# Weight conversion of the first MoE layer placed behind the gate steps of its first six units

## The chip, the cores and the metric

The kernel runs on one core of one Trainium2 chip. The metric is the device time of one execution in microseconds (us); the kernel before was run three times, and its median is 710.7 us (707.14 to 711.53).

## The reference

Three layers follow one another. Clustered attention over 2 x 8 heads of 768 tokens gives 1536 tokens of 512 numbers. Then come two feed-forward layers ("MoE" layers); the first is the one around the change:

```
h = x @ w_in                      # 1536 x 512 times 512 x 2048
P = a[0] + a[1]*h + a[2]*h^2 + a[3]*h^3
Q = 1 + |b[0]|*|h| + |b[1]|*h^2
g = P / (Q + 1e-06)
x = g @ w_out                     # 1536 x 2048 times 2048 x 512
```

The second layer is x @ w_in2, a softmax-weighted product with a layer norm, and a product with w_out2. The weights of both layers arrive as float64.

## The kernel before

**Units.** The first MoE layer is cut into 48 units, each one block of 512 tokens (j) and one block of 128 hidden columns (f). Units 0 to 7 take j = 0 and f = 0 to 7, units 8 to 15 the same f for j = 1, units 16 to 31 all sixteen f for j = 2, units 32 to 47 f = 8 to 15 for j = 1 and then j = 0. A unit is made of five pieces:

- `ff_h` (line 710): TensorE (PE) makes h, 12 matmuls into one PSUM bank (128x512, names h0, h1, ...). There are four such banks, so the h of unit u + 4 can begin only when the bank of unit u is free. That is after `y L750` of unit u, which reads it last.
- `ff_g1` (line 732), the first gate step: ScalarE (ACT) makes t = |h| (L734) and y = a3*h + a2 (L735), GpSimd (POOL) makes q from t in two operations (L736, L737), VectorE (DVE) two operations on y and h (L738, L739).
- `ff_g2` (line 742): ACT takes Ln (L745) and Exp (L746) of q, writing over the h bank, and DVE finishes the quotient in three operations (L748, L749, L750).
- `ff_g3` (line 752): ACT rounds y to gh (L755), POOL makes the rest gl = y - gh (L756).
- `ff_y` (line 761), two units later (LAG = 2): PE adds gh and gl times w_out to four PSUM banks, again 12 matmuls. Two of them use gh alone and stand ahead of the first that needs gl.

**Weights.** Each block f of weights is 128 x 1024 numbers: columns 0 to 511 are for `ff_h`, 512 to 1023 for `ff_y`. It is converted in two halves, half 0 and half 1. One half goes through `to_f32` and `to_parts`: a transfer of 512 KB into a raw tile (L118), two ACT operations (L128 and L131), one DVE operation that puts the pieces together (L135), one ACT rounding (L139, the tile w1h) and one POOL difference (L140, the tile w1l). `to_f32` and `w1_parts` are generators that stop at each `yield`; four steps are one half. Blocks 0 to 4 (NPRE = 5) are converted during attention. Blocks 5 to 11, 14 halves in all, are converted during the first units: `bg` is the list of their generators, `run_bg(4)` (line 699) takes four steps. The raw tiles rotate through three buffers (`cv1`), the joined tiles w1w through two (`cw`).

**What sets the order.** Each engine works through its own queue in order. The order in the queue is set by the compiler's scheduler, which lists an instruction when its own estimate of time says that it is ready, in the order of the program otherwise. The program can hold instructions back with edges of order alone: `tc.issue_after(ins)` queues everything that its block puts on the engine of `ins` behind `ins`, and leaves other engines and the DMA queue (SP) free.

The main loop before the change is this:

```python
run_bg(4)
...
for u in range(NU + LAG):
    if 1 <= u <= NU:
        ff_g2(u - 1)
    if u < NU:
        hp = ff_h(u)
        ff_g1(u, hp)
    if 1 <= u <= NU:
        ff_g3(u - 1)
    ...
    if u >= LAG:
        ff_y(u - LAG)
    run_bg(4)
```

Of the kernel before, what the change touches and what calls it, by code (L numbers as in the profile page):

```python
# [10 lines left out]
AF = mybir.ActivationFunctionType  # L11
# [19 lines left out]
def fused_kernel(ctx: ExitStack, tc: tile.TileContext, qT, kT, v, cent, w1, w2i, w2o, gln, coef, centT, cst, out):  # L31
    nc = tc.nc
# [51 lines left out]
    NPRE = 5  # L84
# [18 lines left out]
    cv = [None]  # L103
# [9 lines left out]

    def to_f32(w, src, nm, early=False):
        raw = cv[0].tile([128, 512], mybir.dt.uint64, name=f"raw{nm}", tag="raw")
        nc.sync.dma_start(out=raw, in_=src)  # L118
        yield
        words = raw.bitcast(U32).rearrange("p (n two) -> p n two", two=2)  # L120
        lo, hi = words[:, :, 0], words[:, :, 1]
        wf, wu = w, w.bitcast(U32)

        nc.scalar.activation(out=wf, in_=hi.bitcast(F32), func=AF.Prelu, scale=2.0 ** -112, alpha=-(2.0 ** 32))  # L128


        nc.scalar.activation(out=lo, in_=lo, func=AF.Identity, scale=2.0 ** -29 * (1 - 2.0 ** -16), bias=less)  # L131
        if early:
            yield
        yield
        nc.vector.scalar_tensor_tensor(wu, wu, 3, lo, op0=ALU.logical_shift_left, op1=ALU.bitwise_or)  # L135
        yield
# [28 lines left out]
    raw, vv = {}, {}  # L165
    last = {}
# [528 lines left out]
    a0, a1, a2, a3 = (coef_t[:, i:i + 1] for i in range(4))  # L695
# [3 lines left out]
    def run_bg(k):  # L699
        while k and bg:  # L700
            try:
                next(bg[0])
                k -= 1
            except StopIteration:
                bg.pop(0)
# [26 lines left out]
    def ff_g1(u, hp):  # L732
        t, q, y = T("t", u), T("q", u, bufs=2), T("y", u, bufs=3)
        nc.scalar.activation(out=t, in_=hp, func=AF.Abs)  # L734
        nc.scalar.activation(out=y, in_=hp, func=AF.Identity, scale=a3, bias=a2)  # L735
        nc.gpsimd.tensor_scalar(q, t, ab[:, 1:2], ab[:, 0:1], op0=ALU.mult, op1=ALU.add)  # L736
        nc.gpsimd.tensor_tensor(q, q, t, op=ALU.mult)  # L737
        nc.vector.tensor_tensor(y, y, hp, op=ALU.mult)  # L738
        nc.vector.scalar_tensor_tensor(y, y, a1, hp, op0=ALU.add, op1=ALU.mult)  # L739
        live[u] = (q, y, hp)  # L740
# [167 lines left out]
    NTT = TOK // 128  # L908
    LAG = 2
    NU = len(ff_units)  # L910
    run_bg(4)
    turn[0] += turn[0] % 2
    h2 = []
    for u in range(NU + LAG):
# [4 lines that stand above are left out]
# [10 lines left out]
            h2.append(t_h(order[u - NU]))  # L929
        if u >= LAG:  # L930
            ff_y(u - LAG)
        run_bg(4)

    run_bg(10 ** 6)
    m1.close()
# [57 lines left out]
```

## Time and profile before

| what | value |
|---|---|
| median of three runs | 710.7 us |
| the profiled execution, its own time | 709.8 us |
| span of that execution in the trace | 708.0 us |
| PE busy | 624.2 us, 88% of the span |
| DVE busy | 500.0 us, 71% |
| ACT busy | 437.8 us, 62% |
| POOL busy | 393.2 us, 56% |
| PE's share of the chain that ended last | 35% |
| first matmul of the first MoE layer | at 273.35 us |
| first matmul of the second MoE layer | at 553.74 us |

The profile is one execution recorded on the chip. Times in it count from the start of the span. A row gives an engine, the line of the kernel, the operation with what it writes and reads, and how often. The idle time of an engine just before a row is put down to the instruction (its releaser) that ended it. The granted clock is the share of TensorE's full clock that the chip gave: 1.00 stands for 2.4 GHz and 0.50 for 1.2 GHz. The shares of busy time are means over attention and two MoE layers with different limits, so what this change is worth has to be read in its own stretch, from 273 us on.

### The profile page before, as it was taken

Reading aid. Unit: us, or ns where it says so; the run is one execution under the profiler, and the core shown is the slowest. Engines: PE = TensorE matmul, PEld = TensorE weight load, DVE = VectorE, ACT = ScalarE, POOL = GpSimd, SP = SyncE. Lnnn points to the kernel's source line nnn. Section 1 sums busy time; section 2 is a strip of 40 time slices with the busy share of each in tenths; the row PEclk is TensorE's granted clock in tenths of the full one; section 3 lists DMA queues with packets and bytes.
Section 4 is the critical chain, followed back from the end, with each engine's and each line's share of the span. In section 5 each row is a group of like instructions: output and inputs, shape, how many; then the busy total and the mean of one; then the engine's idle time right before and its main releaser. Section 6 shows DMA issues by size and latency. Waiting matters only on the chain.

```text
span 708.0 us, 13757 instructions
## 1 busy us (share of the span) xinstructions
PE 624.2 (88%) x5517; PEld 493.4 (70%) x5517; DVE 500.0 (71%) x648; ACT 437.8 (62%) x796; POOL 393.2 (56%) x363
## 2 busy tenths in 40 slices
PE   6777888777687868699999999899999899999998
PEld 3555666656466647476888877778888688888887
DVE  4779779788876872889776789878679765444450
ACT  2536556666566664998866798978668434444341
POOL 8554546483848743899765999898579500000000
PEclk9778889899788988799999999999999999999999
DMA  9963393847547224443100144330010000000001
GB/s 242 278 162 85 95 263 91 200 134 193 153 120 190 63 61 140 140 139 107 43 1 0 44 136 124 114 119 1 1 31 0 1 1 15 31 31 15 20 26 44
DMA packets 22439, 64.71 MB, mean 91 GB/s; under 512 B 4532, under 2 KB 5640, under 8 KB 22376
## 3 DMA queue, kind: packets, MB, share of 16 engines
q1 hardware_dynamic: 21944, 63.67, 32.0%
q8 instruction: 43, 0.70, 0.4%
q10 hardware_dynamic: 432, 0.17, 0.1%
q14 instruction: 20, 0.16, 0.1%
HBM read 59.16 MB, written 3.19 MB: 88 GB/s over the span
## 4 chain that ended last, share of the span: by engine, by line
PE 35%; DVE 7%; ACT 7%; DMA 5%; POOL 5%; issue 3%; ACTq 0%; DVEq 0%; POOLq 0%
PE hh L849 9%; PE o L900 9%; PE y L773 8%; PE h L721 6%; DMA raww<-in_w 2%; DMA rawv<-in_w2i 2%; DVE w1w L135 2%; PE lt L882 1%; POOL q L737 1%; POOL gl L756 1%; ACT y L735 1%; ACT h L745 1%; DVE xhl L616 1%; DMA rawv<-in_w2o 1%; ACT t L734 1%
## 5 line engine op out<-in xcount | busy, mean ns | idle before, releaser
L721 PE MATMUL h<-xhl,w1h 128*128 128x512 f32 x384 | 125.3, 404 | 10.8 <-DVE y L750 8.7
L401 ACT ACTIVATE p<-s,m 128x768 f32<-128x768 f32 x96 | 86.1, 898 | 77.8 <-DVE m L388 77.4
L388 DVE TENSOR_REDUCE m<-s 128x1 f32<-128x768 f32 x96 | 89.5, 944 | 40.8 <-PE s L383 40.6
L377 PE MATMUL s<-k,q 128*128 128x384 f32 x192 | 65.7, 429 | 46.3 <-ACT p L401 45.5
L721 PEld LDWEIGHTS h<-xhl,w1h 128*128 128x128 f32 x384 | 74.0, 194 | 29.7 <-DVE y L750 8.1
L428 PE MATMUL pv<-pt,v 32*64 32x192 f32 x3072 | 88.6, 373 | 1.4 <-issue 1.3
L418 DVE STREAM_TRANSPOSE pt<-p 128x1536 f32<-128x1536 f32 x48 | 84.6, 1763 | 0.0
L377 PEld LDWEIGHTS s<-k,q 128*128 128x128 f32 x192 | 34.9, 219 | 69.6 <-ACT p L401 56.3
L428 PEld LDWEIGHTS pv<-pt,v 32*64 32x64 f32 x3072 | 67.5, 153 | 19.4 <-issue 11.1
L773 PE MATMUL y<-gl,w1h 128*128 128x512 f32 x192 | 76.0, 396 | 3.8 <-POOL gl L756 3.8
L756 POOL TENSOR_TENSOR gl<-y,gh 128x512 fp32r<-128x512 f32 x48 | 68.6, 1430 | 18.8 <-ACT gh L755 18.7
L721 PE MATMUL h<-xhl,w1l 128*128 128x512 f32 x192 | 77.3, 404 | 0.0
L773 PE MATMUL y<-gh,w1l 128*128 128x512 f32 x192 | 75.4, 393 | 0.0
L773 PE MATMUL y<-gh,w1h 128*128 128x512 f32 x192 | 69.2, 395 | 0.0
L737 POOL TENSOR_TENSOR q<-q,t 128x512 f32<-128x512 f32 x48 | 64.5, 1344 | 3.2
L738 DVE TENSOR_TENSOR y<-y,h 128x512 f32<-128x512 f32 x48 | 32.9, 685 | 43.0 <-ACT y L735 42.7
L383 PE MATMUL s<-k,q 128*128 128x384 f32 x192 | 57.8, 388 | 2.3 <-DVE k L579 2.3
L736 POOL TENSOR_SCALAR q<-t,ab 128x512 f32<-128x512 f32 x48 | 42.5, 886 | 27.9 <-ACT t L734 19.2
L849 PE MATMUL hh<-vh,xhl 128*128 128x512 f32 x192 | 53.6, 393 | 1.3 <-ACT t L734 1.3
L494 POOL TENSOR_TENSOR xf<-u,rb 128x512 f32<-128x512 f32 (+1 forms) x14 | 13.8, 1006 | 66.0 <-DMA rb<-rd 66.0
L773 PEld LDWEIGHTS y<-gl,w1h 128*128 128x128 f32 x192 | 36.1, 188 | 15.1 <-POOL gl L756 7.2
L745 ACT ACTIVATE h<-q,qc 128x512 f32<-128x512 f32 x48 | 32.9, 685 | 20.0 <-POOL q L737 12.8
(151 smaller groups left out, 1361.0 us busy)
## 6 DMA issues: line engine op xcount, KB each, us to landing
raww<-in_w SPq DMA_DIRECT2D x32, 512.0 KB, 4.5
v<-in_v SPq DMA_DIRECT2D x64, 192.0 KB, 4.7
dup<-in_qT SPq DMA_DIRECT2D x31, 192.0 KB, 5.6
dup<-in_kT SPq DMA_DIRECT2D x31, 192.0 KB, 5.7
rawv<-in_w2i SPq DMA_DIRECT2D x8, 512.0 KB, 3.6
rawv<-in_w2o SPq DMA_DIRECT2D x8, 512.0 KB, 3.5
out<-ob SPq DMA_DIRECT2D x11, 256.0 KB, 2.0
pr<-in_qT SPq DMA_DIRECT2D x7, 384.0 KB, 5.9
```

The costliest lines, as they stand in the source:

```text
L377: r = nc.tensor.matmul(sp[:, a, 0:384], lhsT=q1[i][:, sl], rhs=k1[i][:, a * 384:(a + 1) * 384], start=True, stop=False)
L383: last["pe"] = nc.tensor.matmul(sp[:, a, 0:384], lhsT=q2[i][:, sl], rhs=k2[i][:, a * 384:(a + 1) * 384], start=False, stop=True)
L388: last["dve"] = nc.vector.tensor_reduce(m, sp[:, :, 0:384], axis=AX.XY, op=ALU.min)
L401: last["act"] = nc.scalar.activation(out=P[n, t // 2][:, t % 2], in_=sp[:, :, 0:384], func=AF.Exp, scale=-1.0, bias=m, accum_out=rs[key][: ...
L418: r = nc.vector.transpose(PT[n][:, 2 * i:2 * i + 2].rearrange("p t k -> p (t k)"), p.rearrange("p t a k -> p (t a k)"))
L428: last["pv"] = nc.tensor.matmul(pv[n][64 * c:64 * c + 64, r, 0:192].rearrange("p (t q) -> p t q", t=NT), lhsT=vv[n][sl, j], rhs=PT[n][sl, ...
L721: r = nc.tensor.matmul(hp, lhsT=w[:, kt * 128:(kt + 1) * 128], rhs=x[:, kt], start=(i == 0), stop=(i == 11))
L737: nc.gpsimd.tensor_tensor(q, q, t, op=ALU.mult)
L756: nc.gpsimd.tensor_tensor(gl, y, gh.bitcast(F32), op=ALU.subtract)
L773: nc.tensor.matmul(o, lhsT=w[:, c], rhs=g, start=(first and i == 0), stop=(last and i == 2))
L849: last["th"] = nc.tensor.matmul(hp[:, a], lhsT=y[:, kt], rhs=w[:, 512 * a:512 * a + 512], start=(kt == 0 and e == 0), stop=(kt == 3 and e ...
L900: r = nc.tensor.matmul(op[:, 0:m], lhsT=l[:, kt], rhs=w, start=(n == 0), stop=(n == 23))
```

## The change

Three things are edited. The loading of a raw tile is a function of its own, and the first three loads (both halves of block 5, half 0 of block 6) are issued by themselves ahead of the main loop, where a whole half was converted before (`run_bg(4)`). `ff_g1` notes its second ACT operation in `last["g"]`. And in units 0 to 5, `run_bg(4)` stands in a block that queues its ACT instructions behind that operation of the same unit.

```diff
+    raws = {}
+
+    def load_raw(src, nm):
+        raws[nm] = cv[0].tile([128, 512], mybir.dt.uint64, name=f"raw{nm}", tag="raw")
+        nc.sync.dma_start(out=raws[nm], in_=src)
+
     def to_f32(w, src, nm, early=False):
-        raw = cv[0].tile([128, 512], mybir.dt.uint64, name=f"raw{nm}", tag="raw")
-        nc.sync.dma_start(out=raw, in_=src)
+        if nm not in raws:
+            load_raw(src, nm)
+        raw = raws.pop(nm)
         yield
...
         nc.scalar.activation(out=t, in_=hp, func=AF.Abs)
-        nc.scalar.activation(out=y, in_=hp, func=AF.Identity, scale=a3, bias=a2)
+        last["g"] = nc.scalar.activation(out=y, in_=hp, func=AF.Identity, scale=a3, bias=a2)
...
     NU = len(ff_units)
-    run_bg(4)
+
+
+    for a in range(3):
+        load_raw(w1[NPRE + a // 2, :, 512 * (a % 2):512 * (a % 2) + 512], f"w1{NPRE + a // 2}{a % 2}")
     turn[0] += turn[0] % 2
...
             ff_y(u - LAG)
-        run_bg(4)
+        with tc.issue_after(last["g"].ins) if u < 6 else ExitStack():
+            run_bg(4)
```

The diff moves instructions on all engines from the first unit on; attention before it keeps its order, and so does the DMA queue. In the rows below the number after a name is the unit (t0, y1, q2) or the block and half (w1w50 is block 5, half 0; raww161 block 6, half 1); what stands behind the underscore is a running number. The lines of these operations are 7 higher in the changed kernel.

ACT at the start of the first MoE layer, before, from the second half of block 5 to the Ln of unit 0 (L745):

```order
L131 ACTIVATE raww151_3490<-raww151_3490,less_81 128x512
L139 ACTIVATE w1h5_3457<-w1w50_3459 128x512
L131 ACTIVATE raww160_3531<-raww160_3531,less_81 128x512
L139 ACTIVATE w1h5_3457<-w1w51_3489 128x512
L734 ACTIVATE t0_3480<-h0_3467 128x512
L735 ACTIVATE y0_3482<-h0_3467,coef_72 128x512
L128 ACTIVATE w1w60_3530<-raww160_3531 128x512
L131 ACTIVATE raww161_3584<-raww161_3584,less_81 128x512
L128 ACTIVATE w1w61_3583<-raww161_3584 128x512
L131 ACTIVATE raww170_3637<-raww170_3637,less_81 128x512
L139 ACTIVATE w1h6_3528<-w1w60_3530 128x512
L745 ACTIVATE h0_3467<-q0_3481,qc_3451 128x512
```

ACT at the same place, changed kernel, from its first instruction of the layer to the Exp of unit 0 (L753) and the t of unit 2:

```order
L741 ACTIVATE t0_3476<-h0_3463 128x512
L742 ACTIVATE y0_3478<-h0_3463,coef_72 128x512
L135 ACTIVATE w1w50_3487<-raww150_3457 128x512
L138 ACTIVATE raww150_3457<-raww150_3457,less_81 128x512
L741 ACTIVATE t1_3511<-h1_3498 128x512
L742 ACTIVATE y1_3513<-h1_3498,coef_72 128x512
L752 ACTIVATE h0_3463<-q0_3477,qc_3451 128x512
L135 ACTIVATE w1w51_3524<-raww151_3459 128x512
L138 ACTIVATE raww151_3459<-raww151_3459,less_81 128x512
L146 ACTIVATE w1h5_3485<-w1w50_3487 128x512
L753 ACTIVATE h0_3463<-h0_3463 128x512
L741 ACTIVATE t2_3548<-h2_3535 128x512
```

Seven conversion operations stood ahead of t0 and twelve ahead of Ln of unit 0; now there are none and two.

DVE at the start of the layer, before, up to `L750` of unit 0, which frees the first h bank:

```order
L135 SCALAR_TENSOR_TENSOR w1w50_3459<-w1w50_3459,raww150_3460 128x512
L135 SCALAR_TENSOR_TENSOR w1w51_3489<-w1w51_3489,raww151_3490 128x512
L738 TENSOR_TENSOR y0_3482<-y0_3482,h0_3467 128x512
L135 SCALAR_TENSOR_TENSOR w1w60_3530<-w1w60_3530,raww160_3531 128x512
L739 SCALAR_TENSOR_TENSOR y0_3482<-y0_3482,coef_72,h0_3467 128x512
L135 SCALAR_TENSOR_TENSOR w1w61_3583<-w1w61_3583,raww161_3584 128x512
L738 TENSOR_TENSOR y1_3517<-y1_3517,h1_3502 128x512
L739 SCALAR_TENSOR_TENSOR y1_3517<-y1_3517,coef_72,h1_3502 128x512
L748 SCALAR_TENSOR_TENSOR q0_3481<-q0_3481,h0_3467 128x512
L135 SCALAR_TENSOR_TENSOR w1w70_3636<-w1w70_3636,raww170_3637 128x512
L749 SCALAR_TENSOR_TENSOR h0_3467<-q0_3481,h0_3467 128x512
L750 SCALAR_TENSOR_TENSOR y0_3482<-y0_3482,coef_72,h0_3467 128x512
```

DVE at the same place, changed kernel, up to the same operation (now L757):

```order
L745 TENSOR_TENSOR y0_3478<-y0_3478,h0_3463 128x512
L746 SCALAR_TENSOR_TENSOR y0_3478<-y0_3478,coef_72,h0_3463 128x512
L142 SCALAR_TENSOR_TENSOR w1w50_3487<-w1w50_3487,raww150_3457 128x512
L745 TENSOR_TENSOR y1_3513<-y1_3513,h1_3498 128x512
L746 SCALAR_TENSOR_TENSOR y1_3513<-y1_3513,coef_72,h1_3498 128x512
L142 SCALAR_TENSOR_TENSOR w1w51_3524<-w1w51_3524,raww151_3459 128x512
L755 SCALAR_TENSOR_TENSOR q0_3477<-q0_3477,h0_3463 128x512
L756 SCALAR_TENSOR_TENSOR h0_3463<-q0_3477,h0_3463 128x512
L745 TENSOR_TENSOR y2_3550<-y2_3550,h2_3535 128x512
L757 SCALAR_TENSOR_TENSOR y0_3478<-y0_3478,coef_72,h0_3463 128x512
```

Five joins of weight halves stood ahead of the last gate operation of unit 0; now there are two, and one operation of unit 2 has come in between.

POOL at the start of the layer, before:

```order
L140 TENSOR_TENSOR w1l5_3458<-w1w50_3459,w1h5_3457 128x512
L140 TENSOR_TENSOR w1l5_3458<-w1w51_3489,w1h5_3457 128x512
L736 TENSOR_SCALAR q0_3481<-t0_3480,ab_3449 128x512
L737 TENSOR_TENSOR q0_3481<-q0_3481,t0_3480 128x512
L140 TENSOR_TENSOR w1l6_3529<-w1w60_3530,w1h6_3528 128x512
L736 TENSOR_SCALAR q1_3516<-t1_3515,ab_3449 128x512
L737 TENSOR_TENSOR q1_3516<-q1_3516,t1_3515 128x512
L140 TENSOR_TENSOR w1l6_3529<-w1w61_3583,w1h6_3528 128x512
```

POOL at the same place, changed kernel:

```order
L743 TENSOR_SCALAR q0_3477<-t0_3476,ab_3449 128x512
L744 TENSOR_TENSOR q0_3477<-q0_3477,t0_3476 128x512
L743 TENSOR_SCALAR q1_3512<-t1_3511,ab_3449 128x512
L744 TENSOR_TENSOR q1_3512<-q1_3512,t1_3511 128x512
L147 TENSOR_TENSOR w1l5_3486<-w1w50_3487,w1h5_3485 128x512
L743 TENSOR_SCALAR q2_3549<-t2_3548,ab_3449 128x512
L744 TENSOR_TENSOR q2_3549<-q2_3549,t2_3548 128x512
L147 TENSOR_TENSOR w1l5_3486<-w1w51_3524,w1h5_3485 128x512
L763 TENSOR_TENSOR gl0_3521<-y0_3478,gh0_3520 128x512
L743 TENSOR_SCALAR q3_3602<-t3_3601,ab_3449 128x512
L147 TENSOR_TENSOR w1l6_3576<-w1w60_3577,w1h6_3575 128x512
```

The q of units 0 and 1 now come before the first weight difference, and the weight differences stand about one to a unit.

On PE the order of the first units is h0 to h4, then y of unit 0, h5, the two leading matmuls of y of unit 1, h6, the rest of y of unit 1, y of units 2 and 3, h7, the two leading matmuls of y of unit 4, one matmul of h8, the rest of y of unit 4, then h8 and h9 mixed. Before it was h4, y of unit 0, h5, y of unit 1, h6, y of unit 2, h7, y of unit 3, h8 with y of unit 4, h9. Further on, y of units 16, 17 and 18 come in a row between the first matmul of h21 and the rest of it, where before y of unit 18 stood behind h22. The scheduler's order differs in places through the rest of the first MoE layer too, with the same instructions.

## Rows read from the trace of the kernel before

**Rows 1.** Page, busy times of the engines over the whole span.

```profile
PE 624.2 (88%) x5517; PEld 493.4 (70%) x5517; DVE 500.0 (71%) x648; ACT 437.8 (62%) x796; POOL 393.2 (56%) x363
```

**Rows 2.** Waits of PE from 265 to 600 us: total, times, longest.

```profile
PE h L721 <- DVE y L750: 8.7, 3, 6.5
PE y L773 <- POOL gl L756: 3.8, 7, 0.9
```

**Rows 3.** Timeline of PE: start us, us, operation, idle before and its releaser.

```profile
277.05 0.63 PE L721 MATMUL h<-xhl,w1l 128*128 128x512 f32 x1
...
285.88 0.40 PE L721 MATMUL h<-xhl,w1l 128*128 128x512 f32 x1
...
292.80 1.22 PE L721 MATMUL h<-xhl,w1h 128*128 128x512 f32 x2 [6.52 <-DVE y L750]
...
298.09 0.88 PE L773 MATMUL y<-gh,w1h 128*128 128x512 f32 x2
```

**Rows 4.** Timeline of ACT, DVE and POOL from 277 to 293 us, first conversion to L750.

```profile
277.06 0.67 ACT L128 ACTIVATE w1w<-raww 128x512 f32<-128x512 f32 x1 [3.76 <-DMA raww<-in_w]
...
281.18 0.58 ACT L734 ACTIVATE t<-h 128x512 f32<-128x512 f32 x1
281.66 0.77 ACT L735 ACTIVATE y<-h,coef 128x512 f32<-128x512 f32 x1
...
283.65 1.61 POOL L737 TENSOR_TENSOR q<-q,t 128x512 f32<-128x512 f32 x1
...
285.51 0.62 ACT L139 ACTIVATE w1h<-w1w 128x512 fp32r<-128x512 f32 x1
286.03 0.67 ACT L745 ACTIVATE h<-q,qc 128x512 f32<-128x512 f32 x1
...
288.30 0.59 ACT L746 ACTIVATE h<-h 128x512 f32<-128x512 f32 x1
...
291.99 0.75 DVE L750 SCALAR_TENSOR_TENSOR y<-y,coef,h 128x512 f32<-128x512 f32 x1
```

**Rows 5.** Busy time by stretch: PE, PEld, DVE, ACT, POOL; then granted clock, DMA share, GB/s.

```profile
286.20:292.80 6.60, 0.08 (x2) 0.00 (x1) 4.59 (x6) 6.43 (x12) 5.08 (x5) 0.67 0.44 140
292.80:298.10 5.30, 5.30 (x13) 4.15 (x14) 5.08 (x7) 5.30 (x11) 5.22 (x5) 0.50 0.47 171
298.10:340.00 41.90, 40.04 (x168) 31.08 (x167) 37.63 (x49) 38.11 (x66) 40.26 (x32) 0.99 0.38 126
340.00:400.00 60.00, 60.00 (x263) 48.90 (x262) 41.48 (x61) 42.08 (x70) 39.20 (x34) 1.00 0.00 1
400.00:480.00 80.00, 76.36 (x321) 60.62 (x320) 65.09 (x86) 69.20 (x119) 74.25 (x61) 0.98 0.39 119
```

**Rows 6.** Two shorter waits in PE's timeline, and the clock after each by stretch.

```profile
335.14 0.50 PE L773 MATMUL y<-gl,w1h 128*128 128x512 f32 x1 [0.86 <-POOL gl L756]
...
457.79 0.70 PE L721 MATMUL h<-xhl,w1h 128*128 128x512 f32 x2 [1.97 <-DVE y L750]
...
335.00:337.00 2.00, 1.85 (x8) 1.56 (x9) 1.32 (x3) 2.00 (x5) 1.28 (x3) 1.00 0.80 254
...
459.00:460.00 1.00, 1.00 (x4) 0.79 (x3) 1.00 (x2) 0.81 (x2) 1.00 (x2) 0.53 0.00 0
...
462.00:463.00 1.00, 0.82 (x3) 0.28 (x1) 1.00 (x2) 0.96 (x2) 1.00 (x1) 0.76 0.78 320
```

**Rows 7.** Lines L135, L140, L737, L736, L756 from 276 to 345 us: ns min/median/max.

```profile
L135 DVE SCALAR_TENSOR_TENSOR w1w<-w1w,raww x16: 685/1112/1507, 278.4 to 334.6; 128x512 uint32<-128x512 uint32 x16
...
L140 POOL TENSOR_TENSOR w1l<-w1w,w1h x14: 1263/1300/1754, 280.2 to 330.8; 128x512 fp32r<-128x512 f32 x14
...
L737 POOL TENSOR_TENSOR q<-q,t x11: 1276/1300/1612, 283.7 to 340.0; 128x512 f32<-128x512 f32 x11
...
L736 POOL TENSOR_SCALAR q<-t,ab x11: 761/772/1813, 282.8 to 339.1; 128x512 f32<-128x512 f32 x11
...
L756 POOL TENSOR_TENSOR gl<-y,gh x9: 1287/1735/1749, 296.0 to 343.5; 128x512 fp32r<-128x512 f32 x9
```

## The prediction

> **What bounds the kernel now.** I read the busy times first: PE is busy for 624.2 us, far ahead of DVE, ACT and POOL [rows 1]. These are means over three layers, so I went on to the stretch that the diff moves, the first MoE layer. The table of stretches shows that PE is full there when nothing is late: from 340 to 400 us it is busy for all 60 us and runs 263 matmuls, 0.229 us each [rows 5]. A unit (24 matmuls) then costs 5.5 us, and the layer gets shorter only by what PE loses beside that. The waits of PE from 265 to 600 us name the losses: 8.7 us in three waits for `y L750` on DVE, one of them 6.5 us, and 3.8 us in seven waits for `gl L756` on POOL [rows 2].
>
> The long one is at the start. The last matmul of h3 begins at 285.88, the first of h4 at 292.80 [rows 3]: h4 needs the bank of h0, and `y L750` of unit 0 begins only at 291.99 [rows 4]. Yet h0 was complete at about 277.7 (its last matmul begins at 277.05, 0.63 us long [rows 3]). The timeline of ACT and DVE says where the 14 us between went. t of unit 0 starts at 281.18, 3.5 us after h0, behind the conversions. q is ready at 283.65 + 1.61 = 285.26. Ln follows at 286.03, but Exp only at 288.30, behind two operations of unit 1 and a weight rounding, and L750 at 291.99 [rows 4]. In PE's wait ACT is busy for 6.43 of 6.60 us [rows 5]. So the wait is made by a queue, not by a transfer.
>
> It costs twice: behind it the granted clock is 0.50 (1.2 GHz) from 292.80 to 298.10, for 13 matmuls [rows 5].
>
> **The change part by part.** Nothing is removed or added in work: 14 halves are converted before and after, with the same instructions. What moves is their place.
>
> *The three early transfers.* They have the same places in the DMA queue as before, and the first conversion began at 277.06 when its transfer ended [rows 4]. They are worth nothing by themselves; they make up for the removed `run_bg(4)`, so that the data lies ready when unit 0 asks for it.
>
> *The wait before h4 (first term).* I walk the new queues with durations from rows 4, and 0.1 us less from start to start where one ACT operation follows another (t at 281.18, 0.58 us long, y at 281.66). t0 starts at 277.8 (h0 complete), y0 at 278.3, the two conversion operations at 279.0 and 279.5. t1 must wait for h1, 280.8; y1 281.3. q0 is ready on POOL at about 280.7 (0.8 + 1.3 us behind t0), Ln0 comes behind y1, 282.0. Then two conversion operations and a rounding (282.6, 283.2, 283.8), Exp0 at 284.3, done at 284.9. On DVE L748 and L749 take 0.68 each, to 286.3; one operation of unit 2 stands before L750 (0.69), which runs from 286.9 to 287.65. h4 starts at 287.7 in place of 292.8. PE could have issued it at 285.88 + 0.23 = 286.11. So 6.69 us of loss become 1.6, a gain of **5.1 us**. Bounds: the second weight join stands just before L748 and takes 0.69 to 1.51 us [rows 7]; I have 0.75, so the gain is 4.3 at the least. It is 6.7 if nothing is late.
>
> *The clock behind it (second term).* From 292.80 to 298.09 the 12 matmuls of h4 took 5.29 us [rows 3]; at 0.229 they take 2.75. That is 2.54 us if the clock stays up. Two rows bracket a wait of 1.6 us: after an idle time of 0.86 us the clock stayed at 1.00; after one of 1.97 us it was at 0.53 about a microsecond later and 0.76 in the slice from 462 to 463 [rows 6], some 3.5 us at half speed, a loss of 1.75. My wait lies between them, so I take half of that loss, 0.85, and a gain of **1.7 us** (0.8 to 2.5).
>
> *The stretch behind (third term).* From 298.10 to 340 PE ran 168 matmuls [rows 5], 38.5 us at 0.229, so 3.4 us were lost in small waits and at the tail of the slow clock. The change spreads the 14 halves to about one per unit, up to unit 13. ACT is fine: t, y, Ln, Exp, gh and half a conversion are 3.2 + 2.05 us less eight overlaps of 0.1, 4.5 us of a unit's 5.5. POOL is close: by the medians L736, L737, L756 and L140 take 0.77 + 1.30 + 1.74 + 1.30 = 5.1 us [rows 7]. Walking POOL from the first weight difference (284.55, behind the rounding at 283.8) to half 0 of block 7 gives five L140, four each of the others, 21.7 us, done at 306.3. PE, full from 287.7 (h4, y0, h5, two matmuls, h6, the rest of y1, y2, y3: 84 matmuls, 19.2 us), wants that half for h7 at 306.9. It is just in time. Behind it come L736, L737, another L140 and gl of unit 4: 306.3 + 5.1 = 311.4, wanted at 310.4. That is 1.0 us lost there, and I allow another 0.9 for what such a walk does not see. 3.4 - 1.9 is a gain of **1.5 us**. Bounds: 3.4 if nothing is late; with POOL at its longest durations it turns into a loss (the rival below).
>
> A rule speaks against the change here. The Trainium skill, "GPSIMD Engine Reference", section 1 (Specifications), says that GpSimd shares its SBUF interfaces with VectorE and contends with VectorE instructions that have two SBUF inputs. The trace agrees: L135, with two such inputs, takes 0.69 us at the least and 1.11 in the median, gl 1.29 and 1.74 [rows 7]. By the rule, conversions that lie beside more gate steps keep both engines slow for longer; without it POOL's share of a unit would be its minima, 4.6 us, and the third term 3.4.
>
> *From 400 to 480 us (fourth term).* Blocks 12 to 15 and the second layer's weights are converted there. The scheduler's order differs, the work does not. PE ran 321 matmuls in 80 us, 73.5 at full rate: 6.5 us lost, with POOL busy for 74.25 [rows 5]. New small waits can come and old ones go; the wait of 1.97 us for L750 and its slow clock (3.7 us together) are among them [rows 6]. I take **0**, with 3.7 either way.
>
> *The sum* is 5.1 + 1.7 + 1.5 + 0 = 8.3 us. The profiled execution took 709.8, so 701.5 us; against the median of the runs, 710.7, that is 9.2 less (1.3%). About 1% (7.1 us, a time of 703.6) is what a measurement of this kernel tells from no change.
>
> **The rivals.**
>
> *More goes.* The wait at 457.79 falls too, since PE now makes y of units 16 to 18 together and has other work when a bank is late: 701.5 - 3.7 = 697.8, or 697.0 with the clock kept behind h4. For it: the order on PE there. Against it: POOL's 93% in that stretch. Chance 0.16.
>
> *The wait shrinks, but the rest gives back.* The first term is at its lower end, 4.3, the clock falls for a full 1.75 us, so that the second is 0.8, and the third is 0: 709.8 - 5.1 = 704.7. For it: the wait of 1.6 us is nearer to 1.97 than to 0.86. Against it: ACT has 1 us to spare in each unit. Chance 0.21.
>
> *POOL becomes the bound: slower.* At their longest durations the four operations cost POOL 1.81 + 1.61 + 1.75 + 1.75 = 6.9 us a unit [rows 7], 1.4 above PE's 5.5. Over the eight units 5 to 12 that is 11.2 us, and two falls of the clock add 3.5. The first two terms (6.8) and the 3.4 us lost before, which this replaces, stand against it: 709.8 - 6.8 - 3.4 + 14.7 = 714.3; with the 3.7 us of the fourth term on top, 718.0. It decides as soon as POOL's four operations take over 5.5 us in the mean. For it: the contention above. Against it: from 298.1 to 340 POOL was busy for 40.26 of 41.9 us, with the same halves crowded into it, and PE still lost only 3.4 [rows 5]. Chance 0.06.
>
> *The change does not do what it says.* If t0 were held by a transfer or by memory that is freed late, ACT would do as before: 709.8. For it: t0 is now the first ACT instruction that writes into memory freed by attention. Against it: the first half was written at 277.06, before h0 was complete [rows 4]. Chance 0.05.
>
> **How the numbers follow.** The forecast, 701.5, has 0.52; its own range is 699 to 704. With "more" (0.16) and "gives back" (0.21) the range is **697.0 to 707.0**: at the low end all of the first two terms with the fourth's gain, at the high end "gives back" with a loss of 2.3 in the fourth. It leaves out 0.11 for the last two rivals and some tails. Faster by over 1% means 703.6 or less: the forecast's 0.49, "more" 0.16, and 0.04 of "gives back", 0.69. Within 1%: 0.17 of "gives back", 0.03 of the forecast, 0.05 where nothing happens, and 0.03 from the slower rival, 0.28. Slower: 0.03.
>
> **What would show it.** In the trace of the changed kernel, t0 should start within 0.3 us of 277.8, Exp0 near 284.3, and h4 between 287 and 288.5. The clock behind h4 tells the second term: 1.00 to 294 us and no more than 3.5 us of 0.50. The rows for L140 and L756 between 300 and 320 us tell the third: PE should wait for gl once or twice and under 2 us in all, and h8 and h9 with y of unit 4 should be done near 320 us. It is wrong if PE waits for w1l of block 6 or 7, if POOL's four operations exceed 5.5 us a unit, or if PE's loss from 400 to 480 us moves by more than 3.7.

## The result and the profile after

The changed kernel takes 699.16 us (median of four runs, 697.83 to 701.68), the kernel before 709.5 beside it (four runs, 707.14 to 711.53). The ratio is 0.986 (95% interval 0.9814 to 0.9905), so the change saves 1 to 1.9%. Six later runs (e5 below), beside their own runs of the kernel before, gave 701.03 and 0.9888 (0.9855 to 0.9921). The forecast of 701.5 with the range 697.0 to 707.0 holds both.

The profiled execution of the changed kernel took 697.83 us, with a span of 696.0. Lines stand seven higher than before: `y L750` is now `y L757`, `gl L756` is `gl L763`. First the busy times of the page, to be laid beside [rows 1], and the waits of PE from 265 to 600 us, beside [rows 2]:

```profile
PE 617.4 (89%) x5517; PEld 489.8 (70%) x5517; DVE 497.2 (71%) x648; ACT 437.3 (63%) x796; POOL 393.2 (56%) x363
```

```profile
PE y L780 <- POOL gl L763: 5.5, 7, 2.7
PE h L728 <- DVE y L757: 2.7, 3, 1.5
```

The counts of instructions are the same. The waits for DVE have gone from 8.7 to 2.7 us, the longest from 6.5 to 1.5. The waits for POOL's gl have grown from 3.8 to 5.5, and the longest of them, 2.7 us, is new.

The start of the layer, in PE's timeline (start, duration, operation, idle time before it and its releaser), beside [rows 3]:

```profile
270.40 0.73 PE L728 MATMUL h<-xhl,w1h 128*128 128x512 f32 x2 [1.71 <-ACT w L451]
...
284.84 0.74 PE L728 MATMUL h<-xhl,w1h 128*128 128x512 f32 x2 [1.51 <-DVE y L757]
...
287.73 0.62 PE L780 MATMUL y<-gh,w1h 128*128 128x512 f32 x2
288.86 0.50 PE L780 MATMUL y<-gl,w1h 128*128 128x512 f32 x1 [0.51 <-POOL gl L763]
...
309.25 0.50 PE L780 MATMUL y<-gl,w1h 128*128 128x512 f32 x1 [0.54 <-POOL gl L763]
```

The layer's first matmul starts at 270.40, where before it started at 273.35, so every time of after is 2.95 us early beside one of before. In before's time h4 starts at 284.84 + 2.95 = 287.79 in place of 292.80, and its twelve matmuls take 2.89 us (284.84 to 287.73) in place of 5.29.

The queues that made the wait, in the timeline of ACT and DVE, beside [rows 4]:

```profile
274.99 0.60 ACT L741 ACTIVATE t<-h 128x512 f32<-128x512 f32 x1 [4.65 <-PE h L728]
...
276.15 0.67 ACT L135 ACTIVATE w1w<-raww 128x512 f32<-128x512 f32 x1
...
280.88 0.64 ACT L146 ACTIVATE w1h<-w1w 128x512 fp32r<-128x512 f32 x1
281.40 0.61 ACT L753 ACTIVATE h<-h 128x512 f32<-128x512 f32 x1
...
284.04 0.74 DVE L757 SCALAR_TENSOR_TENSOR y<-y,coef,h 128x512 f32<-128x512 f32 x1
```

ACT now waits for h0 with t0 in hand (idle for 4.65 us before it), and converts behind y0. Exp0 comes at 281.40, 6.4 us behind t0 where 7.1 lay between them before; the larger part of the gain is t0's own start, 274.99 (277.94 in before's time, against 281.18).

By stretch (busy time with counts of PE, PEld, DVE, ACT and POOL; then granted clock, DMA share and GB/s), beside [rows 5]:

```profile
284.84:287.70 2.86, 2.86 (x12) 2.37 (x13) 2.70 (x4) 2.86 (x7) 2.86 (x3) 1.00 0.07 17
298.10:340.00 41.90, 41.36 (x179) 33.38 (x178) 36.02 (x48) 40.38 (x71) 39.78 (x31) 1.00 0.34 114
...
400.00:480.00 80.00, 77.30 (x331) 61.53 (x330) 65.64 (x91) 67.73 (x115) 70.63 (x59) 1.00 0.28 86
537.90:541.00 3.10, 3.09 (x7) 2.48 (x8) 3.10 (x6) 1.40 (x3) 3.02 (x3) 0.50 0.03 5
```

The clock stays at 1.00 (2.4 GHz) behind h4. From 298.1 to 340 us PE runs 179 matmuls in place of 168, from 400 to 480 us 331 in place of 321. But at the end of the layer there is a stretch at 0.50 that before did not have. It stands behind the new wait for gl; here are PE's row and POOL's timeline ahead of it:

```profile
537.91 0.80 PE L780 MATMUL y<-gl,w1h 128*128 128x512 f32 x1 [2.69 <-POOL gl L763]
```

```profile
530.63 3.01 POOL L147 TENSOR_TENSOR vl<-vw,vh 128x512 fp32r<-128x512 f32 x2
533.63 1.19 POOL L743 TENSOR_SCALAR q<-t,ab 128x512 f32<-128x512 f32 x1
534.91 1.27 POOL L744 TENSOR_TENSOR q<-q,t 128x512 f32<-128x512 f32 x1
536.14 1.71 POOL L763 TENSOR_TENSOR gl<-y,gh 128x512 fp32r<-128x512 f32 x1
```

PE waits for the gl that starts at 536.14. ACT had its gh ready at 534.4 (a rounding of 0.62 us that begins at 533.82); POOL was still working off two weight differences of the second layer (vl, 3.01 us) and a later unit's two operations on q.

**Where the time went.** In both traces I counted PE's matmuls from the first of the layer to the first of the second layer (the product on line 849 of before, hh), and split the layer at the same counts. Each trace holds all 1152 matmuls of h and y (the last 36 stand behind the second layer's first), so the counts are the same; a split at 480 is the start of the matmul behind the 480th. In both traces the clock is at 0.50 for a part of the first 5 us of the layer, so they compare like with like.

| part of the first MoE layer | before, us | after, us | gain |
|---|---|---|---|
| first matmul to h4 | 19.45 | 14.44 | 5.0 |
| h4's twelve matmuls | 5.29 | 2.89 | 2.4 |
| from there to the 480th matmul | 100.28 | 98.94 | 1.3 |
| 480th to 840th | 89.30 | 86.90 | 2.4 |
| 840th to the second layer's first | 66.08 | 68.32 | -2.2 |
| the layer | 280.39 | 271.48 | 8.9 |

The span is 12.0 us shorter. Of the rest, 2.95 us lie ahead of the layer, in attention, whose queues the change leaves as they were: it ended 2.95 us sooner. That is chance. In the profiles of the experiments below the layer's first matmul starts anywhere from 269.76 to 275.38 us. So I judge a kernel by its layer, from its own first matmul on, and by the ratio of its runs.

### The profile page after: what moved, and what is told of

Same layout as the page of the kernel before. It is cut to its first block, busy times and chain, and to the rows that moved or that the text cites. A ratio compares the mean times of both kernels' runs of the same rounds, so it can differ in the third digit from the quotient of the medians.

```text
span 696.0 us, 13772 instructions
## 1 busy us (share of the span) xinstructions
PE 617.4 (89%) x5517; PEld 489.8 (70%) x5517; DVE 497.2 (71%) x648; ACT 437.3 (63%) x796; POOL 393.2 (56%) x363
## 4 chain that ended last, share of the span: by engine, by line
PE 36%; POOL 11%; ACT 7%; DVE 4%; issue 3%; DMA 1%; ACTq 0%; POOLq 0%; DVEq 0%
PE hh L856 9%; PE o L907 9%; PE y L780 8%; PE h L728 7%; POOL q L744 3%; POOL gl L763 2%; POOL q L743 2%; POOL vl L147 2%; PE lt L889 2%; ACT h L752 1%; POOL w1l L147 1%; ACT t L741 1%; ACT y L742 1%; DVE w1w L142 1%; ACT w1h L146 1%
## 5 line engine op out<-in xcount | busy, mean ns | idle before, releaser
L728 PE MATMUL h<-xhl,w1h 128*128 128x512 f32 x384 | 123.0, 397 | 4.4 <-DVE y L757 2.7
L728 PEld LDWEIGHTS h<-xhl,w1h 128*128 128x128 f32 x384 | 72.6, 190 | 22.1 <-DVE y L757 4.0
L435 PE MATMUL pv<-pt,v 32*64 32x192 f32 x3072 | 85.8, 363 | 0.2 <-issue 0.2
L384 PEld LDWEIGHTS s<-k,q 128*128 128x128 f32 x192 | 34.4, 217 | 70.3 <-ACT p L408 54.4
L763 POOL TENSOR_TENSOR gl<-y,gh 128x512 fp32r<-128x512 f32 x48 | 66.6, 1387 | 10.6 <-ACT gh L762 10.4
L745 DVE TENSOR_TENSOR y<-y,h 128x512 f32<-128x512 f32 x48 | 32.8, 683 | 34.1 <-ACT y L742 34.0
L390 PEld LDWEIGHTS s<-k,q 128*128 128x128 f32 x192 | 41.2, 222 | 2.6 <-issue 2.6
```

The costliest lines, as they stand in the source:

```text
L384: r = nc.tensor.matmul(sp[:, a, 0:384], lhsT=q1[i][:, sl], rhs=k1[i][:, a * 384:(a + 1) * 384], start=True, stop=False)
L390: last["pe"] = nc.tensor.matmul(sp[:, a, 0:384], lhsT=q2[i][:, sl], rhs=k2[i][:, a * 384:(a + 1) * 384], start=False, stop=True)
L435: last["pv"] = nc.tensor.matmul(pv[n][64 * c:64 * c + 64, r, 0:192].rearrange("p (t q) -> p t q", t=NT), lhsT=vv[n][sl, j], rhs=PT[n][sl, ...
L728: r = nc.tensor.matmul(hp, lhsT=w[:, kt * 128:(kt + 1) * 128], rhs=x[:, kt], start=(i == 0), stop=(i == 11))
L763: nc.gpsimd.tensor_tensor(gl, y, gh.bitcast(F32), op=ALU.subtract)
```

## The experiments

My theory is that the place of the conversion in ACT's queue makes the gain, by the wait before h4 and the clock behind it, and that the transfers add nothing by themselves. The rivals: the early transfers do it; the removed `run_bg(4)` ahead of the loop does it; or spreading the halves does it, by taking load off POOL later. A second question is what the new wait at the layer's end costs. All diffs are against the changed kernel. Runs that share the runs of before stand between lines. A star marks a layer whose first matmuls ran at full clock; where they did not, as in the first profiles of before and after, the 47 matmuls behind the layer's first start 1.6 us later (12.53 to 12.55 against 10.95 to 10.99 us), so layers compare star with star.

| kernel | median, us (runs) | ratio to before (95% interval) | layer, us | idle before h4, us |
|---|---|---|---|---|
| e1: early transfers, no edges | 710.42 (10) | 0.9998 (0.9969 to 1.0028) | 282.61 * | 7.09 |
| e2: edges, no early transfers | 702.87 (4) | 0.9874 (0.9841 to 0.9906) | 275.07 | 3.76 |
| e3: nothing converted behind unit 0 | 705.97 (6) | 0.9919 (0.9885 to 0.9953) | 275.54 * | 1.19 |
| e4: two more operations on ACT | 704.64 (9) | 0.9929 (0.9901 to 0.9957) | 276.43 | 2.56 |
| --- | | | | |
| e5: the changed kernel again | 701.03 (6) | 0.9888 (0.9855 to 0.9921) | 270.16 * | 1.66 |
| e6: edges for units 0 to 2 | 706.16 (12) | 0.994 (0.9909 to 0.9971) | 277.98 * | 1.67 |
| e7: edges for all 14 halves | 694.93 (6) | 0.9798 (0.977 to 0.9827) | 267.76 | 1.50 |
| e8: last half of the second layer late | 695.91 (6) | 0.9814 (0.9784 to 0.9844) | 266.79 * | 1.65 |
| --- | | | | |
| e9: unit 1's half behind Exp0 | 697.65 (6) | 0.9847 (0.9802 to 0.9892) | 270.39 | 0.46 |
| e10: e7 and e8 | 694.77 (6) | 0.9801 (0.9765 to 0.9838) | 266.31 * | 1.63 |
| e11: e7, e8 and e9 | 694.92 (6) | 0.9799 (0.976 to 0.9839) | 266.16 * | 0.44 |

**e1, the early transfers alone.** The edges go, the three early transfers stay.

```diff
-        with tc.issue_after(last["g"].ins) if u < 6 else ExitStack():
-            run_bg(4)
+        run_bg(4)
```

> Early loads without the edges of order: the first three raw tiles are loaded ahead and the half that was converted ahead of unit 0 is converted in unit 0, but nothing holds the conversion behind a gate step. The scheduler then lists every instruction on every engine in the order of the kernel before. Theory (the place of the conversion on ScalarE makes the gain): 709.5 us like before, h4 again idle 6.5 us behind L750 of unit 0 with a clock of 0.50 behind it. Rival (the early transfers make the gain): 699 to 703 us, idle under 2 us. The start of the first MoE layer, 273.35 us before and 270.40 us in the changed kernel with the same order of instructions up to there, also tells how far attention differs from one execution to the next: a start within 0.5 us of 273.35 speaks for a hidden effect of the change on attention, one 2 us or more away from it for chance.

The ratio is 0.9998. The wait and the slow clock are those of before (PE's timeline, and the stretch behind it):

```profile
290.44 0.80 PE L728 MATMUL h<-xhl,w1h 128*128 128x512 f32 x1 [7.09 <-DVE y L757]
```

```profile
290.40:295.70 5.30, 5.26 (x12) 4.18 (x13) 5.13 (x7) 5.30 (x10) 5.22 (x5) 0.50 0.53 179
```

The scheduler put every queue in the order of before: on each of the four engines the traces of e1 and before hold the same operations in the same order. So the early transfers are worth nothing alone, and the removal of `run_bg(4)` isn't either: without edges the first half still went ahead of t0. The layer starts at 272.00, between the two marks that the expectation set, and is 2.2 us longer than before's in spite of the star: the parts behind h4 take 101.50, 91.16 and 66.22 us, where before took 100.28, 89.30 and 66.08. With the same order, then, a part of a single profile can differ by some 2 us.

**e2, the edges without the early transfers.** `run_bg(4)` stands ahead of the loop again.

```diff
-    for a in range(3):
-        load_raw(w1[NPRE + a // 2, :, 512 * (a % 2):512 * (a % 2) + 512], f"w1{NPRE + a // 2}{a % 2}")
+    run_bg(4)
```

> The edges of order without the early loads: one half is converted ahead of unit 0 as before, then the conversion of units 0 to 5 is held behind the gate step. Theory (what stands ahead of t0 on ScalarE counts): t0 waits for the first transfer, two conversion operations and a rounding and starts about 2 us later than in the changed kernel, L750 of unit 0 about 1.1 us later, so idle 2.5 us before h4, and the clock falls for some 3.5 us; together 2.8 us more than the changed kernel, 702.0 us. Rival (the edges alone do it, the place of the first half is worth nothing): 699.2 us, idle 1.5 us. From unit 19 on its order on PE is that of the changed kernel: if the second conversion stretch gains by its order, it does so here too, about 2.9 us against before.

```profile
286.45 0.79 PE L728 MATMUL h<-xhl,w1h 128*128 128x512 f32 x1 [3.76 <-DVE y L757]
```

```profile
286.40:291.50 5.10, 5.05 (x12) 3.99 (x13) 4.46 (x7) 4.96 (x10) 5.10 (x5) 0.50 0.30 104
```

The edges alone take the wait from 6.52 to 3.76 us, not to the 2.5 that I expected, and the clock falls behind it all the same. The layer is 3.6 us longer than after's. So the two parts of the change work together: with the half gone from ahead of t0 as well, the wait is 1.51 us, and the clock stays up. From the 480th matmul to the 840th PE has after's order and takes 86.81 us, after 86.90, before 89.30: the gain of that stretch, 2.9 us by the expectation, comes here too.

**e3, nothing converted behind unit 0.**

```diff
-            run_bg(4)
+            run_bg(4 if u else 0)
```

> As the changed kernel, but no conversion in unit 0: the first half is converted in unit 1. Theory: two conversion operations leave the queue ahead of t1, but VectorE's join of that half now stands just before L748 of unit 0; idle before h4 1.2 us in place of 1.5, clock 1.00, all weights one unit later but still in time: 698.9 us. Rival (GpSimd has no slack left, every half that comes later is paid): PE waits for w1l of block 5, 6 or 7, 1 to 3 us more than the changed kernel, 700 to 702 us.

The idle time before h4 is 1.19 us, as expected, and the layer is 5.4 us longer than e5's, which has a star too. PE's timeline says where:

```profile
309.24 0.50 PE L728 MATMUL h<-xhl,w1l 128*128 128x512 f32 x1 [0.42 <-POOL w1l L147]
...
322.82 0.73 PE L728 MATMUL h<-xhl,w1h 128*128 128x512 f32 x2 [1.32 <-DVE y L757]
...
348.13 0.50 PE L780 MATMUL y<-gl,w1h 128*128 128x512 f32 x1 [1.23 <-POOL gl L763]
```

PE waits 0.42 us for a weight (w1l), and up to the 480th matmul 4.2 us for gl and for h banks (after 1.3). The rival's cost came, larger than its 1 to 3 us and for the most part by another path than the one it named: there is no slack of one half. The forecast's walk of POOL, which ended "just in time" for half 0 of block 7, had the same answer.

**e4, two more operations between Ln0 and Exp0.** Two copies of q0 into a tile that nothing reads; the computation is otherwise whole.

```diff
+        if u == 0:
+            e = m2a.tile([128, 512], F32, name="extra", tag="extra")
+            for _ in range(2):
+                x = nc.scalar.activation(out=e, in_=q, func=AF.Copy)
+                behind(x, d)
+                d = x
```

> As the changed kernel, with two more ScalarE operations (128x512, 0.63 us each) between Ln and Exp of unit 0, into a tile that nothing reads. It lengthens the wait before h4 alone. Theory A (the clock falls for a wait between 1.5 and 2.0 us): idle 2.5 us, the clock at 0.50 for some 3.5 us from about a microsecond after h4 has begun, 1.0 + 1.75 = 2.8 us more than the changed kernel, 702 us. Theory B (the clock falls only for waits well above 2 us, and the fall at 459 us of the kernel before had another cause): idle 2.5 us, clock 1.00, 1.0 us more, 700.2 us.

```profile
289.28 1.22 PE L728 MATMUL h<-xhl,w1h 128*128 128x512 f32 x2 [2.56 <-DVE y L765]
```

```profile
286.70:289.28 2.58, 0.02 (x2) 0.01 (x1) 2.55 (x5) 2.58 (x5) 1.16 (x3) 0.88 0.61 194
289.28:290.30 1.02, 1.02 (x3) 0.84 (x4) 0.89 (x2) 1.02 (x3) 1.02 (x2) 0.50 0.00 0
290.30:294.00 3.70, 3.70 (x14) 2.98 (x13) 3.27 (x5) 3.53 (x8) 3.70 (x4) 0.76 0.45 142
```

The wait grew by 1.05 us, two operations. The clock fell too: h4's twelve matmuls took 4.17 us in place of 2.89, 1.28 more. The two together are 2.3 us, where theory A expected 2.8. About half of the 1.28 is back two matmuls later, since after waits 0.51 us for gl there and e4 does not. So an operation ahead of Exp0 costs its own length, and the second term of the forecast stands on whether the wait stays short. The rest of the 5.0 us by which this layer is longer than after's is not from here: the order further on is another one, with three waits of 0.92 to 1.65 us between 431 and 456 us.

**e5, the changed kernel again.** No edit.

> The changed kernel itself once more, as the reference for the runs beside it. The first MoE layer, from its first matmul to the first of the second layer, should again take 271.5 us within 1 us, the wait before h4 1.5 us with the clock at 1.00 behind it, and the wait near the layer's end 2.7 us. Its start, 270.4 us in the first trace, may lie anywhere from 269.7 to 275.4 as in the runs so far. Time 699 to 701 us.

Idle time, walk and end of the layer repeat, with a wait of 2.70 us for gl. The layer is 1.3 us shorter than in the first profile, 0.3 more than expected, because PE ran the first matmuls at full clock: from 270.5 to 275 us it was at 0.63 there and is at 1.00 here. This difference is chance. From h4 on the parts repeat within 0.2 us: 2.89, 98.94, 87.07 and 68.21.

**e6, edges for units 0 to 2 only.**

```diff
-        with tc.issue_after(last["g"].ins) if u < 6 else ExitStack():
+        with tc.issue_after(last["g"].ins) if u < 3 else ExitStack():
```

> As the changed kernel, with the edges of order in units 0 to 2 only in place of 0 to 5. ScalarE's queue is the same up to Ln of unit 1. Theory (the gain of the first units is made at unit 0): the wait before h4 again 1.5 us, the first 60 matmuls within 0.5 us of 17.3 us; the order behind unit 2 is the scheduler's own, and the later parts may move by up to 3 us either way: 697 to 702 us. Rival (the later edges are needed too): conversion crowds the gates again in units 3 to 8, so from the 60th to the 240th matmul it takes 45 us like before instead of 42.9: over 702 us.

The wait before h4 is as short as after's, but the layer is 7.8 us longer than in e5. PE's timeline and VectorE's:

```profile
310.78 0.50 PE L728 MATMUL h<-xhl,w1h 128*128 128x512 f32 x1 [1.33 <-DVE xhl L623]
...
314.22 0.50 PE L728 MATMUL h<-xhl,w1h 128*128 128x512 f32 x1 [2.00 <-DVE xhl L623]
```

```profile
306.74 1.68 DVE L623 TENSOR_TENSOR xhl<-xf,xhl 128x512 fp32r<-128x512 f32 x1 [0.31 <-ACT xhl L336]
308.35 1.77 DVE L142 SCALAR_TENSOR_TENSOR w1w<-w1w,raww 128x512 uint32<-128x512 uint32 x1
310.04 0.68 DVE L623 TENSOR_TENSOR xhl<-xf,xhl 128x512 fp32r<-128x512 f32 x1
```

Without the later edges the remaining halves come early, in a bunch. Their joins (L142) stand on DVE between the pieces of the next token block's split (L623), which h8 needs. The rival holds, and more: from the 60th matmul to the 240th it takes 48.66 us where 45 were foretold, 3.3 of them idle behind DVE. The bunch loses where I hadn't looked for it, on DVE, and not on POOL. So the short wait before h4 does not make the gain alone; without the edges of units 3 to 5 about half of it is lost again (706.16 us against 701.03 beside it and 710.6 of before).

**e7, edges for all 14 halves.**

```diff
-        with tc.issue_after(last["g"].ins) if u < 6 else ExitStack():
+        with tc.issue_after(last["g"].ins) if u < 14 else ExitStack():
```

> As the changed kernel, with the edges in units 0 to 13, all that convert blocks 5 to 11. Theory (unit 0 decides): the first 60 matmuls the same 17.3 us, the rest the same within what a new order does (up to 3 us): 697 to 702 us. Rival (each unit that is held gains): from the 60th to the 480th matmul 97 us or less in place of 98.9: under 697 us.

It beats the changed kernel, 694.93 against 701.03 us beside it, and lies below the range of the theory, but not where the edges stand: from the 60th matmul to the 480th it takes 98.97 us, after 98.94. So the time is the rival's and the reason is not. The gain is at the layer's end: from the 1080th matmul on it takes 8.23 us, after 13.12, and no wait of 2.7 us is there.

**e8, the last half of the second layer's weights late.** The changed kernel, with the `to_parts` of the last block, and so its two weight differences on POOL, held behind the gl that the program issued last before it (unit 45).

```diff
-            to_parts(h[:, o], l[:, o], w)
+            with tc.issue_after(last["gl"].ins) if i == 7 else ExitStack():
+                to_parts(h[:, o], l[:, o], w)
```

(`last["gl"]` is set in `ff_g3`.)

> As the changed kernel, with one more edge: the two GpSimd operations that end the conversion of the last weight block of the second layer (L147, vl7) are queued behind gl of unit 44. Nothing else moves but these two, from ahead of q of unit 46 to behind gl of unit 45. Theory (the wait of 2.69 us near the layer's end is made by these two operations on GpSimd): gl of unit 44 ends about 2 us earlier, the wait falls to 0.6 us and the clock does not fall behind it, a gain of 3.5 us over the changed kernel: 695.7 us. Rival (gl of unit 44 waits for its gate steps anyway, or the wait only moves to the next gl): within 1 us of the changed kernel.

```profile
536.23 0.50 PE L780 MATMUL y<-gl,w1h 128*128 128x512 f32 x1 [0.62 <-POOL gl L763]
```

695.91 us were measured, 5.1 less than the changed kernel beside it. The wait at the layer's end is 0.62 us, the clock behind it 1.00 (536.2 to 541 us). On PE the order is after's up to the second layer's first matmul. So the end of the layer does cost after some 3.4 us, wait and slow clock together (a layer of 266.79 against 270.16 in e5), made by two weight differences of 3 us that stood in POOL's queue ahead of a gl whose gh was ready.

**e9, unit 1's half behind Exp0.** Two conversion operations fewer stand ahead of Exp0.

```diff
-        with tc.issue_after(last["g"].ins) if u < 6 else ExitStack():
+        with tc.issue_after(last["e" if u == 1 else "g"].ins) if u < 6 else ExitStack():
```

(`last["e"]` is set at Exp in `ff_g2`.)

> Edit: the changed kernel, but the conversion of unit 1 is issued behind Exp of unit 0 on ScalarE in place of its own first gate step, so that two conversion operations fewer (1.1 us) stand ahead of Exp0. Theory A (what is left of the wait before h4, 1.5 us, is the queue on ScalarE, walked operation by operation): the idle time of PE before h4 falls to about 0.4 us, the clock stays at 1.00, and the 60th matmul starts about 1.1 us sooner after the layer's first than in the changed kernel with the same clock in h0 (17.3 there with h4 at 14.4, 15.9 to 16.1 with h4 at 13.0). Theory B (VectorE or h1 holds h4 as well, the queue is not what counts at this size): the idle time stays above 1.0 us. What the layer makes of it behind unit 12 is the scheduler's new order and not foretold closer than 3 us: 266 to 271 us for the layer by A.

```profile
284.58 0.73 PE L728 MATMUL h<-xhl,w1h 128*128 128x512 f32 x2 [0.46 <-DVE y L757]
289.13 0.50 PE L780 MATMUL y<-gl,w1h 128*128 128x512 f32 x1 [1.03 <-POOL gl L763]
```

The idle time falls by 1.1 us, as the walk of the queue has it. Yet the next wait, for gl, grows from 0.51 to 1.03, and from h4's start to the 480th matmul it takes 103.0 us, after and e5 101.8. The 1.1 us are given back within the next 100 us, in waits for gl: 2.4 us in all from h4's end to the 480th matmul, 1.3 in after. 697.65 us is not to be told from the changed kernel with this many runs.

**e10 and e11, the edits together.** e10 is e7 and e8; e11 adds e9.

```diff
+            with tc.issue_after(last["gl"].ins) if i == 7 else ExitStack():
+                to_parts(h[:, o], l[:, o], w)
...
+        with tc.issue_after(last["g"].ins) if u < 14 else ExitStack():
```

```diff
+        with tc.issue_after(last["e" if u == 1 else "g"].ins) if u < 14 else ExitStack():
```

> Edit: edges for all 14 halves (as in the kernel of 694.9 us) and the last half of the second layer's weights held behind gl of the last unit but a few (as in the kernel of 695.9 us). Theory A (both take away the same wait of 2.7 us at the end of the layer): their gains don't add, about 695 us, no wait over 1 us for gl in the last 20 us of the layer. Theory B (they work in two places): the gains add, 694.9 - (699.2 - 695.9) = about 691.6.

> Edit: all three edits at once: unit 1's conversion behind Exp of unit 0, edges for all 14 halves, the last half of the second layer's weights late. Theory A: as the kernel with the two last edits, less the 1.1 us before h4: about 694 us, idle time before h4 about 0.4 us. Theory B (the idle time before h4 isn't made by the queue): as that kernel, about 695 us, idle time above 1.0 us.

694.77 and 694.92 us: e7 and e8 take away the same wait and don't add, and e9's edit brings nothing on top, with an idle time of 0.44 us before h4. The four kernels from 694.8 to 695.9 us can't be told apart; against before, their ratios of 0.980 to 0.981 stand beside 0.986 and 0.989 for the changed kernel, some 3 to 6 us less. Each beats the kernel before. e7 and e8 beat the changed kernel as it ran beside them; e10 and e11 did not run beside it, and their intervals overlap with that of its first four runs.

## Why the prediction was right

It was right in its number and in its first mechanism, and it owes part of the number to terms that cancelled: of the 8.3 us that it summed, 8.9 were found in the layer, by other sizes. The fourth term, taken at nothing, gave 2.4 us, and the layer's end, which has no term, took 2.2; that these meet is luck.

**The wait before h4.** 5.1 us were forecast, 5.0 measured. The walk held step by step: t0 at 277.94 in before's time (277.8 forecast), Exp0 at 284.35 (284.3), h4 at 287.79 (287.7). e4 and e9 showed that this queue sets the wait, by an operation's length at a time in either direction, and e1 that the transfers don't.

**The clock behind it.** 1.7 us were forecast, 2.4 measured. The step that was mis-sized is "I take half of that loss": for a wait between 0.86 and 1.97 us I priced half a fall. There is none behind 1.51 us, nor behind the wait before h4 in any of e3 and e5 to e11 (0.44 to 1.67 us). e4, with 2.56 us, paid 1.3 us. So at this place the wait either kept the clock or cost 1.3 to 2.4 us of it (2.4 in before, e1 and e2), and the 0.85 of the sum is neither. Of the 2.4 us, 0.5 go at once into PE's wait for gl at 288.86, which counts in the third term.

**The stretch behind.** 1.5 us were forecast, 1.3 measured; e1's part, in before's order, is 1.2 us longer than before's, so the size is not known closer than that. Beside the 0.51 behind h4, PE waited for gl once between 300 and 320 us, 0.54 us at 309.25, for the gl that the walk gave a delay of 1.0. What speaks of POOL's share are the groups of lines from 274 to 345 us (count, busy time, mean ns):

```profile
L147 POOL TENSOR_TENSOR w1l<-w1w,w1h 128x512 fp32r<-128x512 f32 x14 | 20.9, 1495 | 1.2 <-ACT w1h L146 1.2
L744 POOL TENSOR_TENSOR q<-q,t 128x512 f32<-128x512 f32 x13 | 17.5, 1346 | 0.8
...
L763 POOL TENSOR_TENSOR gl<-y,gh 128x512 fp32r<-128x512 f32 x11 | 15.1, 1376 | 0.0
...
L743 POOL TENSOR_SCALAR q<-t,ab 128x512 f32<-128x512 f32 x13 | 12.1, 933 | 13.5 <-ACT t L741 12.0 <-DVE h L756 1.2 <-ACT y L742 0.3
```

The four means make 1.50 + 1.35 + 1.38 + 0.93 = 5.2 us a unit, under the 5.5 at which POOL would have decided: the slower rival did not come. PE waited for no weight, and h8, h9 and y of unit 4 were done at 317.03, 319.98 in before's time (320 forecast). The two operations by which the forecast weighed the Trainium skill's rule on shared interfaces ("GPSIMD Engine Reference", section 1, Specifications) got shorter, not longer:

```profile
L763 POOL TENSOR_TENSOR gl<-y,gh x11: 1282/1295/1752, 287.5 to 344.1; 128x512 fp32r<-128x512 f32 x11
...
L142 DVE SCALAR_TENSOR_TENSOR w1w<-w1w,raww x15: 681/831/1470, 277.7 to 342.2; 128x512 uint32<-128x512 uint32 x15
```

The medians fell from 1735 to 1295 ns and from 1112 to 831 [rows 7] (972 where the stretch ends as far from the layer's start as in rows 7); the longest stayed. But the weight difference on POOL got longer, in the mean from 1389 ns (L140 in before, 276 to 345 us) to the 1495 above, and the four means together were 5.3 us in before. In before, gl took 1.29 to 1.30 us where neither L135 nor the split (L616) ran on DVE beside it, and 1.73 to 1.75 where one did, which is in line with that rule of the Trainium skill. In after 2 of 11 gl take over 1.7 us, where 6 of 9 did, but 6 of 14 weight differences, where 3 of 14 did. So "both engines slow for longer", which the forecast drew from the rule, did not come: some operations got shorter, others longer, and POOL's share of a unit hardly moved.

**From 400 to 480 us.** 0 was taken, with 3.7 either way; 2.4 came (480th to 840th matmul). The longest waits there are now 0.85 and 0.73 us where 1.97 stood [rows 6], and the clock stays at 1.00. This is what the rival "more goes" said would happen, and it came for the most part; the time stayed near the forecast because the layer's end took 2.2 us back. It goes with the order: the five profiles with after's order on PE there (after, e2, e3, e5, e8) take 86.8 to 87.1 us, the two with before's order 89.3 and 91.2. Whether the rival's own reason does, y of units 16 to 18 made together, is not shown: these run from 378 to 387 us, and the wait of 1.97 us was for h32, which comes 58 us behind them in after. "Gives back" did not come, since neither of the first two terms was at its lower end, and t0 at 274.99 excludes that the change did nothing.

**The layer's end.** The prediction has no term for it. The scheduler's order changes up to there, 250 us behind the last edge, and its new order of POOL cost a wait of 2.69 us and a slow clock. e8, which has after's order on PE up to there, put its price at 3.4 us (a layer of 266.79 against 270.16 in e5).

Of the difference between the forecast and the profiled execution, 701.5 - 697.8 = 3.7 us, 3.0 is the chance start of the layer and 0.6 the layer itself.

**What stays open.** Why the order far behind an edit comes out better or worse I can't say: e2, e3 and e4 have a wait of about 2.7 us at the layer's end as after has, e7 and e9 do not, and I could only see it in each order. e9's 1.1 us go into waits for POOL's gl, but which instruction of the queues makes them was not tried.

## What to carry to other kernels

Where work that isn't urgent shares an in-order queue with the chain that frees a buffer, count what stands ahead of that chain's first instruction and between its steps, and move it behind the first step; on the bound engine this pays twice when the wait gets short enough for the clock to stay up. Move no more than there is slack for, and neither bunch the work again behind that place (e6) nor start it late (e3). After an edit that a scheduler answers with a new order, read the whole stretch it reorders to its end, measured from a landmark of its own: here the largest cost left over, some 3.4 us, lay 250 us behind the edit and was taken away by one further edge.

## What was not expected of the hardware

**The clock and the length of a wait.** Before h4 the granted clock stayed at 1.00 behind every wait from 0.44 to 1.67 us (nine profiles), and was at 0.50 behind every wait from 2.56 to 7.09 us (four profiles). I had expected a gradual cost. Elsewhere in the layer it fell to about half after waits of 1.97 (before), 2.06 (e9, 411.79) and 2.69 us and stayed at 1.00 after one of 0.86. But the length of the single wait does not decide. In e10 and e11 PE waits 1.42 us ahead of the same matmul, by count the 615th of the layer; the 4 us behind it have a clock of 1.00 in e10 and of 0.57 in e11:

```profile
419.81 0.51 PE L780 MATMUL y<-gl,w1h 128*128 128x512 f32 x1 [1.42 <-POOL gl L763]
```

```profile
418.67 0.50 PE L780 MATMUL y<-gl,w1h 128*128 128x512 f32 x1 [1.42 <-POOL gl L763]
```

Ahead of the layer's first matmul stands a wait of 1.71 us in after and in e3; the 4 us behind it have 0.66 in after and 1.00 in e3. A wait of 1.72 us in e6 (427.64) was followed by 0.57. And in e1 a wait of 1.86 us left the clock up, while a second one of 1.82, five us behind it, was followed by 0.63. So that the clock stayed up behind 1.5 us before h4 is what nine profiles show of that place, and no rule for waits of this length. PE's rows of e1 and the stretches behind them:

```profile
457.00 0.70 PE L728 MATMUL h<-xhl,w1h 128*128 128x512 f32 x2 [1.86 <-DVE y L757]
...
462.28 0.50 PE L780 MATMUL y<-gl,w1h 128*128 128x512 f32 x1 [1.82 <-POOL gl L763]
```

```profile
457.00:459.00 2.00, 2.00 (x9) 1.65 (x10) 2.00 (x3) 2.00 (x5) 2.00 (x2) 1.00 0.00 0
462.00:466.00 4.00, 3.72 (x10) 2.98 (x11) 3.69 (x6) 3.25 (x6) 4.00 (x5) 0.63 0.47 140
```

In e6 likewise a wait of 1.33 us left the clock up and one of 2.00, whose matmul starts 3.4 us later, was followed by 0.66.

**The start of the layer.** Attention ended at times up to 5.6 us apart in profiles of kernels whose queues hold the same instructions in the same order up to there; that is more than most effects studied here.
